# A new hand-kept order of 2,562 operations for an attention-then-mixture kernel on one Trainium2 core

## The chip, the core and the metric

One core of a Trainium2 chip runs the whole program. Its engines are TensorE (matrix products into PSUM, PE in the profile, with its weight loads apart as PEld), VectorE (DVE), ScalarE (ACT), GpSimd (POOL) and SyncE (SP), which here only issues transfers. The metric is the device time in microseconds, the median of several runs.

## What is computed

The reference has two parts, for a batch of 8, 8 heads of 64, and 576 positions:

```python
q_d, k_d, v_d = (mean over groups of 4 positions of q, k, v)
out_up = repeat(softmax(q_d k_d^T / 8) v_d, 4)                    # down-sampled attention
out_local = softmax(where(|i - j| < 4, q k^T / 8, -1e9)) v        # local attention
x = (out_up + out_local), heads side by side                      # [8, 576, 512]
logits = x @ w_gate; the two largest of 4 experts, softmax over them -> w
for e in range(4):
    q, k, v = x @ wq[e], x @ wk[e], x @ wv[e]                     # 512 -> 64
    ye = causal_softmax(q k^T / 8) @ v @ wo[e]                    # 64 -> 512
    out += w[e] * ye            # only where e is one of the two
```

## The kernel before

The work is cut into three stages for each batch element b. Stage 1 works on four pairs of heads c: `local` (the local scores, L515, 20 small products of 64x64 tiles), `down` (the down-sampled scores, L588), softmax work on VectorE, ScalarE and GpSimd (L518 to L536 and L591 to L609), transposes `tp` (L383), `o1` and `o1d` (products with v, L650 to L662) and `up` and `x` on VectorE (L667, L670). x is then split into a high and a low part, `xh` (L675) on ScalarE, and `xl` and `xt` (L676, L678) on VectorE or GpSimd. For b = 0 the down-sampled v is made on TensorE (`vd_mm`, L573), for the others on VectorE or GpSimd (`vd`, L567 and L568). Stage 2 projects x to q, k and v by dense 128-row products in three parts, high by high, high by low and low by high (L693, L739, L748; for q of b = 0 and its first pair of experts pair by pair at L708), and stage 3 does the causal attention and the output (L852 to L1011). Results leave PSUM by copies at L325 (ScalarE) and L327 (VectorE).

Each operation is written once as an entry of a plan, with the engines that may do it ("GV": GpSimd or VectorE; "AV": ScalarE or VectorE). A table of numbers, `SEQ`, decides everything else: the number divided by 4 says which operation comes next, the rest says which of its engines takes it, and -1 stands for a warm-up, a product of zeros (L472) that writes a PSUM buffer which nobody reads. Each engine gets its instructions in the order of the table and keeps it; it waits only for what an instruction needs. Seven more warm-ups (L360) stand ahead of the table.

```python
        for x in SEQ:
            o = self.ops[x // 4] if x >= 0 else self.filler()
            o.which = x % 4 if x >= 0 else 0
            o.who = o.eng[o.which]
            out.append(o)
```

TensorE products on plain float32 tiles of 64 rows (stage 1, scores, and the products with v) are issued as two passes each, so an operation of 20 such products is 40 matmuls and 40 weight loads in the trace; transposes and the dense products are issued once.

Of the kernel before, what the change touches and what calls it, by code (L numbers as in the profile page):

```python
# [17 lines left out]
    0, 173, 2112, 4, 177, 24, 136, 140, 189, -1, 192, 197, 120, 268, -1, 124, 232, -1, -1, -1, -1, -1, 200, 20,  # L18
    1148, 144, 64, 84, 92, 236, 149, 152, 240, -1, 204, 208, 244, 272, 88, 96, -1, -1, -1, 285, -1, -1, -1, -1, -1,
    -1, -1, -1, 288, 292, 156, 160, 164, 169, 220, 416, 8, 12, 68, 72, 296, 216, 413, 180, 185, 376, 380, 301, 304,  # L20
    76, 214, 312, 320, 429, 364, 16, 80, 572, 248, 316, 324, 384, 432, 437, 252, -1, -1, 128, 132, 360, 532, 536,
    440, 256, 328, 332, 336, 340, 260, 344, 308, 388, 540, -1, 568, 392, 464, 468, 348, 353, 264, 445, 28, 48, 52,
    356, 504, 544, 396, 400, 404, 773, 448, 408, -1, -1, 276, 280, 508, 776, 456, 460, 585, 588, 736, 740, 592, 744,
    720, 472, 476, 548, 40, 44, 480, 484, 552, 488, 556, 516, 224, 724, 228, 420, 32, 454, 620, 596, 424, 624, 708,
    897, 560, 748, 752, 492, 601, 604, 610, 36, 612, 617, 520, 712, 840, 844, 784, 788, 793, 796, 628, 632, 368,
    372, 576, 580, 56, 636, 564, 660, 664, 668, 672, 812, 756, 848, 760, 901, 909, 640, 496, 500, 801, 804, 852,
    764, 768, 644, 648, 656, 652, 810, 912, 1061, 512, 996, 676, 680, 60, 684, 688, 816, 1024, 1028, 1065, 917, 856,
    920, 925, 692, 696, 704, 781, 1032, 876, 880, 884, 936, 940, 944, 832, 524, 948, 1073, 1076, 1080, 1084, 528,
    952, 956, 960, 1000, 716, 1196, 1237, 700, 888, 1036, 964, 1200, 860, 1204, 904, 1208, 1088, 864, 868, 872, 928,
    968, 1092, 1040, 1044, 892, 1168, 100, 112, 104, 1332, 1336, 836, 1233, 1049, 972, 980, 1508, 828, 824, 820,  # L30
    1069, 1212, 1216, 1220, 1052, 1340, 1056, 1224, 1228, 976, 1152, 1156, 728, 732, 1172, 1008, 1012, 1513, 984,
    988, 1436, 934, 1098, 1160, 992, 1108, 1112, 1100, 1104, 1245, 1248, 1548, 1552, 1556, 1560, 1252, 1256, 1261,
    1432, 1753, 1564, 1004, 1460, 1464, 1568, 1572, 1468, 1756, 1576, 1264, 1268, 1580, 1164, 1272, 1277, 1292,
    1344, 1180, 1520, 1524, 1116, 1120, 1124, 1496, 1472, 1476, 1528, 1532, 1348, 1352, 1128, 1132, 1136, 1480,
    1537, 1540, 1356, 1544, 1484, 1488, 1384, 1284, 1500, 1296, 1288, 1300, 1176, 1184, 1360, 1364, 1368, 1592,
    1388, 1504, 1584, 1144, 1492, 1588, 1648, 1644, 2073, 1241, 1141, 1596, 1608, 1612, 1600, 1604, 1304, 1308,
    1312, 1316, 1616, 1392, 1396, 1765, 1768, 1320, 1716, 1328, 1324, 1620, 1624, 1720, 1728, 1016, 1020, 1400,
    1404, 1408, 2077, 1773, 1776, 1724, 1780, 1784, 1672, 1676, 1412, 1416, 1516, 1790, 1372, 1376, 1820, 2128,
    1680, 1732, 1736, 1740, 1744, 1420, 1424, 1280, 1429, 117, 1380, 1824, 2132, 1828, 1832, 2016, 1708, 1629, 1792,
# [1091 lines left out]
```

## Time and profile before

| | us |
|---|---|
| median of 3 runs (453.13 to 455.3) | 453.43 |
| span of the profiled execution | 451.9 |
| TensorE busy | 441.2 |
| VectorE busy | 362.5 |
| ScalarE busy | 346.1 |
| GpSimd busy | 301.2 |

The profiled execution is one more run; of its own time the profile gives the span, from the first to the last instruction, which lies 1.5 us under the median of the runs. The ends of matmuls are modelled, so that a TensorE that the profile calls busy can still be slower than at its best; idle time of an engine that others wait for is what costs.

### The profile page before, as it was taken

The page shows a single profiled execution, that of the slowest core. Times are in us where ns is not written, and L with a number is a line of the kernel's source. Part 1 is how long each engine was busy: PE and PEld are TensorE (multiplying, and loading weights), DVE is VectorE, ACT ScalarE, POOL GpSimd, SP SyncE. Part 2 cuts the span into 40 slices and gives each one's busy share as a digit, 9 for nine tenths or more (in the row PEclk, how much of TensorE's full clock was granted, in tenths as well). Part 3 has the DMA queues.
Part 4 walks back from the last instruction along what each step waited for, and adds up shares of the span by engine and source line. Part 5 has one row for each costly group of instructions (what it writes and reads, how often), then busy time and mean ns, then how long its engine had stood idle before and what let it go on. Part 6 is the DMA issues. An engine that isn't in the chain of part 4 may idle for free.

```text
span 451.9 us, 20317 instructions
## 1 busy us (share of the span) xinstructions
PE 441.2 (98%) x8374; PEld 401.8 (89%) x8375; DVE 362.5 (80%) x1020; ACT 346.1 (77%) x1099; POOL 301.2 (67%) x485
## 2 busy tenths in 40 slices
PE   8998999999999999999999999999999999999997
PEld 4787999989999889998899898999999999998876
DVE  8997989896859999777988999895897768445782
ACT  7985899687968898756867888775997687456783
POOL 6997878768867888665764776765984863304320
PEclk9998999999999999999999999999999999999999
DMA  8966537433344544543334432443272200200113
GB/s 251 281 191 188 169 99 212 123 112 83 89 141 137 155 126 136 158 141 89 113 108 160 118 99 65 133 140 92 62 220 63 70 1 4 80 28 14 52 57 106
DMA packets 44300, 52.70 MB, mean 117 GB/s; under 512 B 4144, under 2 KB 27184, under 8 KB 44208
## 3 DMA queue, kind: packets, MB, share of 16 engines
q1 hardware_dynamic: 44208, 51.40, 38.1%
q8 instruction: 66, 1.08, 1.0%
q14 instruction: 26, 0.21, 0.1%
HBM read 40.90 MB, written 9.44 MB: 111 GB/s over the span
## 4 chain that ended last, share of the span: by engine, by line
PE 87%; DVE 4%; DMA 4%; issue 2%; SPq 1%; ACT 1%; DVEq 0%; ACTq 0%
PE pj L693 20%; PE pv L739 10%; PE po L989 10%; PE sq L852 9%; PE o L966 8%; PE tq L383 6%; PE tp L383 5%; PE sc L515 4%; PE o L650 4%; PE scd L588 3%; DMA lv<-in_v_dram 3%; PE pv L748 2%; PE o L657 2%; PE po L1011 1%; PE o L970 1%
## 5 line engine op out<-in xcount | busy, mean ns | idle before, releaser
L875 ACT ACTIVATE pr<-pr,pst 128x384 f32<-128x384 f32 (+8 forms) x144 | 80.0, 558 | 13.3 <-DVE pst L872 12.6
L883 POOL TENSOR_SCALAR pr<-pr,pst,gt 128x64 f32<-128x64 f32 (+8 forms) x97 | 65.9, 687 | 16.2 <-DVE pst L880 12.0
L693 PE MATMUL pj<-xh,wqk_h 128*128 128x320 f32 (+1 forms) x248 | 74.8, 302 | 0.0
L693 PE MATMUL pj<-xh,wqk_l 128*128 128x320 f32 (+1 forms) x248 | 72.8, 293 | 0.0
L693 PE MATMUL pj<-xl,wqk_h 128*128 128x320 f32 (+1 forms) x248 | 72.7, 293 | 0.0
L872 DVE CUSTOM_DVE_ANT_0 pr<-sq,causal_t 128x384 f32<-128x384 f32 (+8 forms) x144 | 63.8, 484 | 5.2 <-PE sq L852 4.7
L852 PE MATMUL sq<-k,q 64*64 64x256 f32 (+6 forms) x768 | 52.2, 370 | 0.0
L693 PEld LDWEIGHTS pj<-xh,wqk_h 128*128 128x128 f32 x248 | 46.5, 188 | 2.5 <-issue 0.6
L693 PEld LDWEIGHTS pj<-xh,wqk_l 128*128 128x128 f32 x248 | 46.5, 188 | 0.0
L693 PEld LDWEIGHTS pj<-xl,wqk_h 128*128 128x128 f32 x248 | 46.5, 187 | 0.0
L978 POOL TENSOR_TENSOR ol<-oc,oh 128x256 fp32r<-128x256 f32 (+1 forms) x27 | 22.1, 822 | 32.4 <-ACT oh L977 22.6
L852 PEld LDWEIGHTS sq<-k,q 64*64 64x64 f32 x768 | 32.9, 133 | 7.0 <-issue 0.3
L598 ACT ACTIVATE dp<-scd,dst 128x144 f32<-128x144 f32 x96 | 35.2, 376 | 3.4 <-DVE dst L593 2.7
L739 PE MATMUL pv<-wvg_h,xh 128*128 128x260 f32 x128 | 37.0, 289 | 0.0
L739 PE MATMUL pv<-wvg_l,xh 128*128 128x260 f32 x128 | 36.1, 282 | 0.0
L739 PE MATMUL pv<-wvg_h,xl 128*128 128x260 f32 x128 | 36.1, 282 | 0.0
L676 POOL TENSOR_TENSOR xl<-x,xh 128x576 fp32r<-128x576 f32 x22 | 32.4, 1473 | 4.5 <-ACT xh L675 4.0
L536 POOL TENSOR_TENSOR lp<-lp,lst 128x640 f32<-128x640 f32 x24 | 31.9, 1336 | 4.4 <-DVE lst L535 3.7
L383 PE MATMUL tq<-ident,pr 64*128 64x64 f32 x736 | 33.2, 228 | 1.4 <-DVE pst L872 0.6
L989 PE MATMUL po<-oh,wo_h 128*128 128x256 f32 (+1 forms) x112 | 34.0, 304 | 0.0
L989 PE MATMUL po<-oh,wo_l 128*128 128x256 f32 (+1 forms) x112 | 33.0, 294 | 0.0
L383 PEld LDWEIGHTS tq<-ident,pr 64*128 64x128 f32 x736 | 27.1, 138 | 6.5 <-issue 2.6
(182 smaller groups left out, 1438.8 us busy)
## 6 DMA issues: line engine op xcount, KB each, us to landing
lv<-in_v_dram SPq DMA_DIRECT2D x64, 160.0 KB, 3.7
lq<-in_qT_dram SPq DMA_DIRECT2D x32, 292.0 KB, 3.5
lk<-in_kT_dram SPq DMA_DIRECT2D x32, 292.0 KB, 3.9
out_dram<-ot SPq DMA_DIRECT2D x28, 288.0 KB, 2.3
lr<-in_v_dram SPq DMA_DIRECT2D x28, 256.0 KB, 3.2
lr<-in_v_dram SPq DMA_DIRECT2D x56, 32.0 KB, 3.0
wst<-in_wqk_dram SPq DMA_DIRECT2D x1, 1024.0 KB, 9.1
vx<-vg SPq DMA_DIRECT2D x8, 128.0 KB, 2.6
```

Source lines behind the costliest of these rows:

```text
L383: T.transpose(ps()[:, 512 * x + z[x]:512 * x + z[x] + 64], data[r, 0:128], ident[r, r])
L536: op("l_nrm", "GV", (pool_tt(n), dve(n)), lambda e: eng[e].tensor_tensor(p(), p(), st[:, :, 2:3].to_broadcast([128, NT, W]), op=OP.mult), ...
L598: A.activation(p()[:, t, :], scs()[:, at * t:at * t + SD], AF.Exp, bias=st[:, t, 4:5], scale=1.0 / 128.0, accum_out=st[:, t, 0:1])
L676: op("xl", "GV", (1360, dve(576)), lambda e: eng[e].tensor_tensor(xl(), x(), xh()[:, 0:S].bitcast(F32), op=OP.subtract), r=[x, (xh, 0)], w ...
L693: T.matmul(ps()[:, H0 + n0:H0 + n1], ww[:, c, w0 + 128 * p:w0 + 128 * p + 128], xx[b, c]()[:, n0:n1], start=(i == 0), stop=(i == 3 * NP - 1))
L739: T.matmul(ps()[:, at:at + 260], xx[b, c]()[:, 128 * t:128 * t + 128], ww[:, c, :], start=(i == 0), stop=(i == 3 * NP - 1))
L852: T.matmul(pss[x][0]()[halves[e ^ turned(t)], at_of[x] + at + to:at_of[x] + at + to + n1 - n0], q()[r, 64 * t:64 * t + 64], k()[r, n0:n1], ...
L872: op("s_max", "V", dve(n) + 4, lambda x=x, t=t, n=n, src=src: V.tensor_tensor_reduce(rows_of[t], src(), causal_t[:, S - 64:S + 256] if t = ...
L875: op("s_exp", "A", 281 + n / 1.2, lambda x=x, t=t, n=n: A.activation(rows_of[t], rows_of[t], AF.Exp, bias=st[:, x, 4:5], scale=-1.0, accum ...
L883: op("s_nrm", "GV", (327 + n / 1.2 + max(0, n - 384) * 1.1, 189 + n / 1.92), lambda g, x=x, t=t, n=n: eng[g].tensor_scalar(rows_of[t], row ...
L966: T.matmul(obs[x]()[r, q0:q1], vg()[kr, j, 64 * (2 * p + e):64 * (2 * p + e) + 64], pt()[kr, e, j, q0:q1], start=j == 0, stop=j == len(job ...
L989: T.matmul(ps()[:, H1 + n0:H1 + n1], ww[:, p, 128 * c:128 * c + 128], xx[b, p]()[:, n0:n1], start=(i == 0), stop=(i == 5))
```

## The change

Only the table `SEQ` changes. It has 2,562 entries in place of 2,586: the same operations, in a new order, and none of the 24 entries of -1. Of the operations, 202 go from the first engine of their list to the second, 142 from the second to the first, and 14 otherwise to or from a third. With the table seven lines shorter, line numbers after it are seven lower in the changed kernel.

```diff
 SEQ = (
-    0, 173, 2112, 4, 177, 24, 136, 140, 189, -1, 192, 197, 120, 268, -1, 124, 232, -1, -1, -1, -1, -1, 200, 20,
+    4, 0, 136, 177, 124, 173, 120, 220, 8, 12, 140, 216, 188, 192, 197, 144, 272, 269, 232, 16, 236, 360, 284, 200,
...
```

The choices of engine that move most: s_nrm (L883) from 97 on GpSimd and 47 on VectorE to 84 and 60; q_ev (the copy of q out of PSUM) from 13 on ScalarE and 3 on VectorE to 6 and 10; wo_ev (the copy of the output) from 28 and 8 to 20 and 16; v_ev from 14 and 2 to 11 and 5; xl from 22 on GpSimd and 10 on VectorE to 19 and 13; xt from 29 and 3 to 21 and 11; o_lo (L978) from 27 and 5 to 21 and 11; kd (L551 on VectorE, with L553) from 18 on GpSimd and 14 on VectorE to 13 and 19; and the other way vd from 17 on GpSimd and 11 on VectorE to 21 and 7, and qd from 13 and 19 to 17 and 15.

The first place is TensorE's queue at the very start, from the first local scores (`sc`) on. Before, warm-ups (`wu`) stand between them:

```order
L515 MATMUL sc<-lk,lq 64x64 x20
L588 MATMUL scd<-kd,qd 64x144 x6
L472 LDWEIGHTS zero
L472 MATMUL wu<-zero 128x512
L472 LDWEIGHTS zero
L472 MATMUL wu<-zero 128x512
L515 MATMUL sc<-lk,lq 64x64 x20
```

And now:

```order
L508 MATMUL sc<-lk,lq 64x64 x20
L581 MATMUL scd<-kd,qd 64x144 x6
L508 MATMUL sc<-lk,lq 64x64 x20
L581 MATMUL scd<-kd,qd 64x144 x6
L566 MATMUL pv<-lv,pool 128x128 x7
L508 MATMUL sc<-lk,lq 64x64 x20
L376 MATMUL tp<-ident,dp 128x64 x10
```

The warm-ups are gone, so that the real work follows directly, and the first `vd_mm` (`pv`) stands ahead of the third local scores; before, it stood behind 19 warm-ups.

The second place is TensorE's queue some 110 instruction rows later, where the last head pair of b = 0 is done (`o_870`, in the new table `o_804`) and the first projection (`pj`) begins. Before:

```order
L650 MATMUL o_870<-pt,lv 64x58 x16
L650 MATMUL o_870<-pt,lv 64x56 x4
L657 MATMUL o_870<-pd,vd 64x144 x4
L660 MATMUL o_870<-pd,vd 64x2x48
L662 MATMUL o_870<-pd,vd 64x48
L660 MATMUL o_870<-pd,vd 64x2x48
L662 MATMUL o_870<-pd,vd 64x48
L515 MATMUL sc<-lk,lq 64x64 x20
L708 MATMUL pj<-xh,wqk_h 128x320
L708 MATMUL pj<-xh,wqk_l 128x320
```

And now:

```order
L566 MATMUL pv<-lv,pool 128x128 x7
L581 MATMUL scd<-kd,qd 64x144 x6
L643 MATMUL o_804<-pt,lv 64x58 x16
L643 MATMUL o_804<-pt,lv 64x56 x4
L508 MATMUL sc<-lk,lq 64x64 x20
L650 MATMUL o_804<-pd,vd 64x144 x4
L653 MATMUL o_804<-pd,vd 64x2x48
L655 MATMUL o_804<-pd,vd 64x48
L653 MATMUL o_804<-pd,vd 64x2x48
L655 MATMUL o_804<-pd,vd 64x48
L701 MATMUL pj<-xh,wqk_h 128x320
L701 MATMUL pj<-xh,wqk_l 128x320
```

The last local scores ahead of the projection have moved in front of the `o1d` products (L657 to L662), and the last `vd_mm` now stands shortly ahead of them.

The third place is SP's queue of loads at the start. Before:

```order
L489 DMA lk<-in_kT_dram 128x584
L488 DMA lq<-in_qT_dram 128x584
L489 DMA lk<-in_kT_dram 128x584
L455 DMA wst<-in_wvg_dram 128x4x260
L489 DMA lk<-in_kT_dram 128x584
L499 DMA lv<-in_v_dram 64x5x128 x2
```

And now:

```order
L482 DMA lk<-in_kT_dram 128x584
L481 DMA lq<-in_qT_dram 128x584
L482 DMA lk<-in_kT_dram 128x584
L481 DMA lq<-in_qT_dram 128x584
L482 DMA lk<-in_kT_dram 128x584
L492 DMA lv<-in_v_dram 64x5x128 x2
```

The load of the weights for v and the gate (`in_wvg`) has left the first six loads; it now stands 13 rows further down, behind the weights for q and k.

## Rows read from the trace of the kernel before

**Rows 1.** The page: span, busy time of each engine, and the instruction queue's transfers.

```profile
span 451.9 us, 20317 instructions
PE 441.2 (98%) x8374; PEld 401.8 (89%) x8375; DVE 362.5 (80%) x1020; ACT 346.1 (77%) x1099; POOL 301.2 (67%) x485
...
q8 instruction: 66, 1.08, 1.0%
```

**Rows 2.** Busy time by stretch: bounds: length, busy (instructions) by engine, clock, DMA share, GB/s.

```profile
0.00:4.50 4.50, 3.20 (x11) 0.95 (x11) 2.94 (x14) 3.71 (x9) 2.95 (x24) 1.00 0.58 182
4.50:22.00 17.50, 16.68 (x338) 11.94 (x339) 16.92 (x36) 14.84 (x53) 15.25 (x25) 1.00 1.06 295
22.00:37.50 15.50, 12.40 (x381) 11.19 (x378) 13.27 (x31) 14.20 (x47) 14.98 (x19) 1.00 0.69 190
37.50:45.00 7.50, 7.50 (x165) 7.08 (x165) 5.40 (x11) 2.80 (x10) 4.88 (x6) 0.77 0.64 182
45.00:100.00 55.00, 55.00 (x1092) 51.09 (x1090) 51.45 (x141) 46.88 (x147) 43.02 (x60) 1.00 0.48 140
100.00:200.00 100.00, 99.94 (x1990) 93.40 (x1989) 82.09 (x233) 81.77 (x267) 77.13 (x125) 1.00 0.43 126
200.00:300.00 100.00, 98.58 (x1917) 91.44 (x1917) 88.06 (x250) 77.18 (x244) 66.17 (x103) 1.00 0.40 121
300.00:400.00 100.00, 99.97 (x1773) 93.48 (x1773) 71.00 (x206) 70.06 (x226) 61.87 (x100) 1.00 0.23 71
400.00:448.60 48.60, 47.80 (x732) 41.20 (x726) 31.39 (x106) 34.26 (x105) 14.94 (x29) 1.00 0.14 50
```

**Rows 3.** TensorE's waits: us in total, times, longest.

```profile
PE sc L515 <- issue: 1.7, 1, 1.7
...
PE tp L383 <- issue: 1.1, 1, 1.1
```

**Rows 4.** TensorE's timeline: start, length, instructions, [idle before <-releaser].

```profile
23.17 0.40 PE L383 MATMUL tp<-ident,lp 64*128 64x64 f32 x5 [1.07 <-issue]
...
37.50 0.56 PE L515 MATMUL sc<-lk,lq 64*64 64x64 f32 x19 [1.68 <-issue]
...
38.55 0.28 PE L708 MATMUL pj<-xh,wqk_h 128*128 128x256 f32 x1
...
39.65 0.42 PE L708 MATMUL pj<-xh,wqk_l 128*128 128x256 f32 x1
```

**Rows 5.** VectorE's timeline at the same two places, and the last `x` of b = 0.

```profile
24.28 0.62 DVE L591 TENSOR_REDUCE scd<-scd 128x3 f32<-128x432 f32 x1 [0.92 <-PE scd L588]
...
38.10 0.82 DVE L518 SCALAR_TENSOR_TENSOR lp<-sc,lmask 128x640 f32<-128x640 f32 x1 [1.83 <-PE sc L515]
...
39.63 0.74 DVE L670 SCALAR_TENSOR_TENSOR x<-up,o 128x576 f32<-128x576 f32 x1
```

**Rows 6.** The page's group of the warm-ups, as TensorE's lines show them.

```profile
L472 PE MATMUL wu<-zero 128*128 128x512 bf16 x23 | 6.2, 381 | 0.4 <-DMA lv<-in_v_dram 0.3 <-PE scd L588 0.2
```

**Rows 7.** VectorE's and GpSimd's groups by shape: busy us, mean ns | idle before.

```profile
L327 DVE COPY q<-pj 128x576 f32<-128x576 f32 x3 | 2.3, 754 | 1.0 <-PE pj L693 1.0
L883 DVE TENSOR_SCALAR pr<-pr,pst,gt 128x256 f32<-128x256 f32 x7 | 3.4, 483 | 0.0
L567 DVE TENSOR_TENSOR lr<-lr 128x512 f32<-128x512 f32 x11 | 8.4, 762 | 0.7 <-DMA lr<-in_v_dram 0.7
L568 DVE TENSOR_TENSOR vd<-lr 128x256 f32<-128x256 f32 x11 | 7.3, 666 | 0.4
```

**Rows 8.** Waits of TensorE's weight loads between 45 and 448 us, the longest two.

```profile
PEld tq L383 <- issue: 2.6, 12, 0.5
PEld sc L515 <- DVE oc L975: 0.9, 1, 0.9
```

**Rows 9.** The chain that ended last, its pieces of load time at the start.

```profile
6.57 8.25 DMA lv<-in_v_dram
14.83 5.00 DMA lv<-in_v_dram
```

273 rows, old and new, of the table SEQ are left out of this document.

## The prediction

> **What bounds the kernel now.** I read the page first: TensorE is busy 441.2 of 451.9 us, 98%, VectorE 80%, ScalarE 77%, GpSimd 67% [rows 1]. A new order cannot take products away, so the gain can only lie where TensorE stands idle, or where it is busy with something that is no work. Next I read the busy time by stretch, to see where that is [rows 2]. Between 45 and 448.6 us TensorE is idle 0.06, 1.42, 0.03 and 0.80 us, together 2.3 us of 403.6. In the first 45 us it is another picture: 16.68 of 17.5 us busy, but with 23 of the 24 warm-ups, worth 6.2 us [rows 6], in it; then 12.40 of 15.5; then 7.5 of 7.5, but at a mean granted clock of 0.77. So the start holds nearly all that is to be had, and it is VectorE's there: 16.92 of 17.5 us busy, then 13.27 of 15.5.
>
> The list of TensorE's waits gives the largest two holes a name: 1.7 and 1.1 us, both with the releaser "issue", which is no other engine [rows 3]. The timeline puts them at 22.1 to 23.17 and 35.82 to 37.50 us, in the middle of one operation each (5 of 10 transposes, 19 of 40 matmuls were still to come) [rows 4], so that no input can be what was missing. 22 + 677 = 699 instructions of TensorE stand before 22.0 us and 1458 before 37.5 us [rows 2]: 759 apart, close to three times 256. The instruction queue made 66 transfers of 1.08 MB together, 16.4 KB each, for 16,749 instructions of TensorE, 254 each [rows 1]. I read both holes as TensorE at the end of a block of instructions whose successor had not come. VectorE feels them at once: it is idle 0.92 us before L591 and 1.83 us before L518 [rows 5].
>
> After the second hole the granted clock falls: in 37.5 to 45 us it is 0.77 in the mean [rows 2], and the same 128x256 product takes 0.28 us at 38.55 and 0.42 us at 39.65 [rows 4]. This is a piece of about 3.4 us at the lower of two levels (1.2 in place of 2.4 GHz), right after 1.68 us of idleness.
>
> **The change, part by part.**
>
> *Holes at block ends in the start.* I counted the new queue, with two passes where the trace has two: the end near instruction 705 falls between transposes and the local scores of b = 1 (small products again), the one near 1473 into the first dense projection, which before came just after it. In the new queue a `vd_mm` of 28 instructions, 128 columns wide, also stands at the start of the block ahead. So I take the second hole as gone, 1.68 us of TensorE that VectorE, with 1.83 us, pays in full, and of the first a third: 2.0 us gained in all. The bounds are 2.75 us gained (both gone, 1.07 + 1.68) and none (two others come).
>
> The Trainium skill, in "Runtime: NRT & Kernel Launch", section "Instruction fetch mechanics", says that crossing into the next block of 256 instructions costs one queue update that is mostly hidden. By that this part would be worth nothing and the sum would end 2.0 us higher. The trace disagrees at two of 65 ends, with 1.07 and 1.68 us, and agrees at most others.
>
> *The lower clock after the second hole.* (1 - 0.77) x 7.5 = 1.7 us of full clock were lost in 37.5 to 45 us, where TensorE is busy throughout [rows 2]. With the hole goes what came before the fall. Gain 1.7 us, bounds 0 and 1.7.
>
> *The 24 warm-ups.* They lie in the stretch where VectorE is busy 16.92 of 17.5 us [rows 2], so their own 6.2 us are hidden behind VectorE, and taking them out gains nothing directly (bounds 0 and the 0.6 us that VectorE is idle there). But without them TensorE is idle more: in 4.5 to 22 us it is busy 16.68 - 6.2 = 10.5 of 17.5 us [rows 2, 6], and the only fall in the trace follows idleness. What this costs is not in the trace of before. From below it is nothing, as VectorE sets the pace; from above all of the work from 4.5 to 37.5 us, 10.5 + 12.4 = 22.9 us, runs at half the clock and takes 45.8 us in place of 33.0, 12.8 us more. Nearest is the one fall seen, 1.7 us; I take two such falls, half of each hidden behind VectorE: 1.7 us lost.
>
> *VectorE's work in the start.* Up to the last `x` of b = 0, which ends at 40.37 us [rows 5], VectorE has 67 operations in place of 64. Out go one xl, one l_nrm, one l_sub, one qd, one vd_ev and some small ones, in come one kd, one qd, one l_max, one vd_ev, two xt and four small ones; by the means of their kinds some 4.7 us go and 4.1 us come. Gain 0.6 us, bounds 0 and 1.2.
>
> *The loads in the start.* The chain of waits runs through the loads of v for 8.25 and 5.00 us [rows 9]. With the 520 KB of `in_wvg` out of the way of the first of them, at 295 GB/s [rows 2] it lands up to 1.8 us sooner; the second has some 230 KB less ahead, 0.8 us. VectorE's queue stands beside it with 16.92 of 17.5 us [rows 2], so I take 0, bounds 0 and 0.8 gained. The weights for v are needed only after the first q and k, and have more than ten microseconds.
>
> *The rest, 45 to 448.6 us.* Gain at most the 2.3 us that TensorE is idle, and something of the waits of its weight loads, the longest group of which is 2.6 us in 12 [rows 8]. Against that stands what VectorE takes over: 7 copies of q and 8 of the output at 0.754 us, 11.3 us; 13 s_nrm at about 0.49 us, 6.4 us; o_lo, xl, xt, kd and v_ev some 14 us; less 4 vd at 0.762 + 0.666 = 1.43 us, 5.7 us, and qd and the sums with eps, some 4 us [rows 7]. That is about 22 us more, 385 of 451.9 us or 85%. It has the room: 355 - 292.6 = 62.4 us idle in 45 to 400 us [rows 2]. The tightest stretch is 45 to 100 us, with 3.55 us free; its share of the 22 us, by its share of VectorE's time (51.45 of 362.5), is 3.1 us. So it stays just under its limit, and I take 1.0 us gained, less than half of the 2.3; bounds 2.3 + 2.6 = 4.9 gained and 3.1 lost, if that stretch has twice its share.
>
> *Sum.* 451.9 - 2.0 - 1.7 + 1.7 - 0.6 - 1.0 = 448.3 us of span; with the 1.5 us by which the median of the runs lies over the profile, 449.8 us.
>
> **The rivals.** *The plan's waits shrink too*: the stretch after 45 us gives its bound, 4.9 us in place of 1.0, and the time is 445.9 us. For it speaks that one wait of 0.9 us there hangs on VectorE behind a long instruction [rows 8]; against it, that VectorE gets more to do, not less.
>
> *No change*: two other block ends fall into small products, the holes and the fall of the clock come again elsewhere (2.0 + 1.7 us back), and the time is 453.5 us. For it speaks that the end near 705 still lies between small products; against it the dense projection at 1473.
>
> *Slower: the clock falls in the start.* With no warm-ups TensorE goes to the lower level again and again until the projections begin. If half of the 22.9 us of work runs there and all of it shows, 11.4 us are lost in place of 1.7, and the time is 459.5 us; from 7.6 us lost on it is slower than before by over 0.5%, and I price this case in the middle, at 457.5 us. For it speaks that idleness of 1.68 us came before the only fall, and that idleness of this size will be common; against it, that TensorE's share of work in 22 to 37.5 us, with hardly a warm-up in it, was 12.40 of 15.5 us at a clock of 1.00 up to its end [rows 2], and that VectorE's queue hides what TensorE loses. The Trainium skill, in "TensorE: Matmul & The Clock Gate", section "What's actually happening", says that the throttled state is the default and that activity releases it; by that this rival is what the missing warm-ups bring, and the fall at 39 us agrees.
>
> **How the numbers follow.** The forecast, about 447.5 to 451.1 us, has 0.40; the shorter waits, 444 to 447.5, 0.16; no change, 451.2 to 455.7, 0.25; the slower start 0.19. 0.5% of 453.43 is 2.3 us, about what a measurement of this kernel can tell from no change, so faster is 0.40 + 0.16 = 0.56, same 0.25, slower 0.19. The range from 444.5 to 456.0 us leaves out the far ends of the second and the fourth case, some 0.05 and 0.13. The forecast by itself is 449.8 us.
>
> **What would show it.** In the profile after: no wait of TensorE on "issue" over 1 us at the start beside at most one; VectorE's wait on the local scores near 38 us gone; the last `x` of b = 0 ending at 36 to 39 us in place of 40.37; the dense projections beginning that much sooner; the granted clock below 1.00 in one or two stretches before 37 us; VectorE near 385 us busy; the rest, from the first projection to the end, as long as before within 2 us. The prediction is wrong if the granted clock stays at half for ten microseconds or more of the start, if new holes on "issue" stand in the stretch after 45 us, or if TensorE there waits for VectorE by several microseconds.

## The result, and the profile after

The changed kernel takes 458.21 us in the median of 12 runs (455.02 to 462.29), the kernel before, beside it on the same chip, 454.32 us. The ratio is 1.0068, interval [1.0042, 1.0095]; in another set of runs (after_2, below) it is 1.0092 [1.0067, 1.0117]. A ratio is worked out from the single runs and leaves out those in a slower state of the chip (here the one of 462.29 us), so that it is not quite the quotient of the two medians. So the change makes the kernel about 0.8% or 3.6 us slower, and the prediction was wrong.

The profiled execution is a long one of the changed kernel's, with a span of 460.0 us; the middle span of the runs is 456.5. The page, by engine, for [rows 1]:

```profile
span 460.0 us, 20255 instructions
...
PE 441.0 (96%) x8351; PEld 401.5 (87%) x8351; DVE 375.8 (82%) x1062; ACT 333.3 (72%) x1075; POOL 288.5 (63%) x466
...
q8 instruction: 66, 1.08, 0.9%
```

VectorE has gained 13.3 us of work, ScalarE and GpSimd have lost about as much each. TensorE is as busy as before, though 24 warm-ups are gone. The same stretches as in [rows 2]:

```profile
4.50:22.00 17.50, 11.24 (x291) 9.77 (x292) 11.97 (x27) 10.94 (x42) 11.56 (x18) 0.92 1.08 274
22.00:37.50 15.50, 14.01 (x377) 12.38 (x379) 14.48 (x36) 13.23 (x41) 12.76 (x14) 0.98 0.80 224
37.50:45.00 7.50, 6.34 (x182) 5.68 (x174) 7.10 (x15) 5.88 (x18) 6.78 (x9) 1.00 0.22 58
45.00:100.00 55.00, 54.18 (x1095) 49.76 (x1090) 53.34 (x137) 43.20 (x142) 42.15 (x58) 1.00 0.44 126
100.00:200.00 100.00, 96.98 (x1827) 89.58 (x1820) 83.57 (x234) 74.30 (x247) 66.03 (x104) 0.98 0.46 129
200.00:300.00 100.00, 99.80 (x1941) 91.65 (x1944) 86.28 (x250) 74.75 (x239) 68.01 (x107) 1.00 0.38 111
300.00:400.00 100.00, 99.41 (x1873) 92.22 (x1866) 80.64 (x232) 72.90 (x241) 61.76 (x104) 1.00 0.29 91
```

Two stretches stand out. In 4.5 to 22 us VectorE does 11.97 us in place of 16.92, though it set the pace there. And between 100 and 200 us TensorE is idle for 3.0 us, where it was idle for 0.06. TensorE's waits, for [rows 3], tell why:

```profile
PE sc L508 <- issue: 3.6, 2, 3.4
PE o L959 <- issue: 1.8, 1, 1.8
PE sc L508 <- DMA lq<-in_qT_dram: 1.4, 1, 1.4
PE pv L566 <- DMA lv<-in_v_dram: 1.2, 1, 1.2
...
PE pj L701 <- issue: 1.0, 1, 1.0
```

The waits on "issue" sum to 6.8 us, with a small one of 0.4; before it was 2.8. TensorE's timeline, for [rows 4], shows the three large ones, each in the middle of an operation (the number in brackets is the idle time before the row, with what ended it):

```profile
14.72 0.57 PE L508 MATMUL sc<-lk,lq 64*64 64x64 f32 x22
18.68 0.50 PE L508 MATMUL sc<-lk,lq 64*64 64x64 f32 x17 [3.39 <-issue]
...
40.45 0.39 PE L701 MATMUL pj<-xl,wqk_h 128*128 128x256 f32 x1 [1.01 <-issue]
...
172.74 0.70 PE L959 MATMUL o<-ptb,vg 64*64 64x320 f32 x3
175.26 2.43 PE L959 MATMUL o<-ptb,vg 64*64 64x320 f32 x27 [1.82 <-issue]
```

The first one is felt on VectorE at once, as in [rows 5]; it has nothing to do for 3.95 us:

```profile
21.03 0.46 DVE L660 TENSOR_REDUCE up<-o 128x144 f32<-128x288 f32 x1 [3.95 <-PE o L655]
```

What was late is seen in the transfers by queue, in 12 to 14 us, first before, then after, and in 16 to 18 us after (packets, MB, share of the 16 engines):

```profile
q1 hardware_dynamic: 566, 0.46, 109.9%
q8 instruction: 1, 0.02, 4.3%
```

```profile
q1 hardware_dynamic: 678, 0.42, 116.4%
```

```profile
q1 hardware_dynamic: 384, 0.75, 102.9%
q8 instruction: 1, 0.02, 3.5%
```

The first block of TensorE's instructions that is fetched during the run (q8) starts at 12.11 us before, at 16.13 us after; TensorE passes the block end after which this fetch comes at about the same time, 7.6 and 8.2 us. All 16 engines are then full of loads, in both. TensorE uses up what it has at 15.0 us and stands until 18.68, that is 2.55 us after the fetch began. Lower clock follows both long waits: 0.92 in 4.5 to 22 us, and 0.83 in 170 to 180 us.

A second profiled execution of the same kernel, after_2 (span 456.2 us, near the middle), has the first fetch at 12.01 us and no wait near 15 us; at 172 us the wait is 0.69 us (a pause of 1.4 us between two weight loads), at 22 to 24 us there is one of 1.1. So the ends of the blocks stay, and what is waited at them changes from one execution to the next. The clock falls here too, in 4.5 to 22 us, with no wait on issue in that stretch:

```profile
4.50:22.00 17.50, 14.41 (x320) 12.57 (x322) 13.41 (x31) 11.36 (x43) 12.37 (x19) 0.80 1.08 267
```

All its waits on issue together are 2.9 us, about the 2.8 of before, and yet its span is 4.3 us longer. The sum of these waits alone therefore doesn't give the loss; where in the run they stand matters too, as the table below shows.

### The profile page after: what moved, and what is told of

Same layout as the page of the kernel before. It is cut to its first block, busy times and chain, and to the rows that moved or that the text cites. A ratio compares the mean times of both kernels' runs of the same rounds, so it can differ in the third digit from the quotient of the medians.

```text
span 460.0 us, 20255 instructions
## 1 busy us (share of the span) xinstructions
PE 441.0 (96%) x8351; PEld 401.5 (87%) x8351; DVE 375.8 (82%) x1062; ACT 333.3 (72%) x1075; POOL 288.5 (63%) x466
## 3 DMA queue, kind: packets, MB, share of 16 engines
q8 instruction: 66, 1.08, 0.9%
## 4 chain that ended last, share of the span: by engine, by line
PE 83%; DVE 7%; issue 3%; POOL 3%; DMA 3%; ACT 1%; SPq 1%; POOLq 0%
PE pj L686 21%; PE po L982 9%; PE pv L732 9%; PE sq L845 8%; PE o L959 7%; PE tq L376 5%; PE tp L376 5%; PE o L643 4%; PE sc L508 4%; PE scd L581 3%; PE pv L741 2%; PE o L650 2%; PE po L1004 1%; DMA lv<-in_v_dram 1%; PE pv L566 1%
## 5 line engine op out<-in xcount | busy, mean ns | idle before, releaser
L868 ACT ACTIVATE pr<-pr,pst 128x192 f32<-128x192 f32 (+8 forms) x144 | 80.1, 560 | 13.2 <-DVE pst L865 12.6
L865 DVE CUSTOM_DVE_ANT_0 pr<-sq,causal_t 128x320 f32<-128x320 f32 (+8 forms) x144 | 64.4, 482 | 9.7 <-PE sq L845 9.3
L876 POOL TENSOR_SCALAR pr<-pr,pst,gt 128x192 f32<-128x192 f32 (+8 forms) x84 | 59.7, 718 | 14.4 <-DVE pst L873 10.9
L529 POOL TENSOR_TENSOR lp<-lp,lst 128x640 f32<-128x640 f32 x23 | 29.5, 1281 | 15.3 <-DVE lst L528 12.7
L845 PEld LDWEIGHTS sq<-k,q 64*64 64x64 f32 x768 | 31.9, 134 | 7.1 <-issue 0.2
L971 POOL TENSOR_TENSOR ol<-oc,oh 128x320 fp32r<-128x320 f32 (+1 forms) x21 | 17.9, 854 | 31.4 <-ACT oh L970 31.4
L959 PE MATMUL o<-ptb,vg 64*64 64x320 f32 (+2 forms) x512 | 32.9, 383 | 1.8 <-issue 1.8
L982 PE MATMUL po<-ol,wo_h 128*128 128x256 f32 (+1 forms) x112 | 32.9, 294 | 0.0
L508 PE MATMUL sc<-lk,lq 64*64 64x64 f32 x1280 | 27.7, 224 | 5.1 <-issue 3.6
```

The costliest lines, as they stand in the source:

```text
L508: T.matmul(sc()[halves[h ^ (t // 5)], 512 * (t // 5) + W * i:512 * (t // 5) + W * i + W], q()[r, z:z + 64], k()[r, z:z + W], start=True, s ...
L529: op("l_nrm", "GV", (pool_tt(n), dve(n)), lambda e: eng[e].tensor_tensor(p(), p(), st[:, :, 2:3].to_broadcast([128, NT, W]), op=OP.mult), ...
L845: T.matmul(pss[x][0]()[halves[e ^ turned(t)], at_of[x] + at + to:at_of[x] + at + to + n1 - n0], q()[r, 64 * t:64 * t + 64], k()[r, n0:n1], ...
L865: op("s_max", "V", dve(n) + 4, lambda x=x, t=t, n=n, src=src: V.tensor_tensor_reduce(rows_of[t], src(), causal_t[:, S - 64:S + 256] if t = ...
L868: op("s_exp", "A", 281 + n / 1.2, lambda x=x, t=t, n=n: A.activation(rows_of[t], rows_of[t], AF.Exp, bias=st[:, x, 4:5], scale=-1.0, accum ...
L876: op("s_nrm", "GV", (327 + n / 1.2 + max(0, n - 384) * 1.1, 189 + n / 1.92), lambda g, x=x, t=t, n=n: eng[g].tensor_scalar(rows_of[t], row ...
```

## The experiments

Four theories. **A**: the loss is waits of TensorE at block ends, and the falls of the clock behind them. **B**: the missing warm-ups cost it. **C**: the engine choices, with VectorE's load. **D**: the new order as such. Each kernel ran in rounds with the kernel before. The profiles are of one execution each. Medians and ratios:

| label | median us | before us | ratio, 95% interval |
|---|---|---|---|
| b_nofill | 453.97 | 454.44 | 0.9993 [0.9965, 1.0021] |
| a_fill | 457.56 | 454.44 | 1.0061 [1.0036, 1.0086] |
| a_tiny | 456.71 | 454.44 | 1.0054 [1.0029, 1.0080] |
| a_choice_b | 516.66 | 454.44 | 1.1391 [1.1337, 1.1444] |
| ba_start | 455.52 | 453.83 | 1.0041 [1.0020, 1.0062] |
| ab_start | 459.04 | 453.83 | 1.0120 [1.0097, 1.0143] |
| a_wless | 456.74 | 453.83 | 1.0063 [1.0037, 1.0090] |
| after_2 | 458.17 | 453.83 | 1.0092 [1.0067, 1.0117] |
| b_split | 457.57 | 455.00 | 1.0049 [1.0020, 1.0077] |
| ba_nofill | 456.39 | 455.00 | 1.0034 [1.0006, 1.0062] |
| ab_fill | 460.36 | 455.00 | 1.0118 [1.0073, 1.0163] |
| a_act | 465.37 | 455.00 | 1.0213 [1.0166, 1.0259] |
| b_split5 | 457.62 | 454.93 | 1.0063 [1.0038, 1.0088] |
| a_split3 | 463.49 | 454.93 | 1.0188 [1.0161, 1.0216] |
| a_split5 | 465.45 | 454.93 | 1.0237 [1.0211, 1.0263] |
| a_best | 466.30 | 454.93 | 1.0262 [1.0231, 1.0292] |
| a_ld | 456.93 | 452.92 | 1.0101 [1.0073, 1.0128] |
| a_mend | 456.52 | 452.92 | 1.0063 [1.0040, 1.0087] |

### The warm-ups

```diff
 SEQ = (
-    0, 173, 2112, 4, 177, 24, 136, 140, 189, -1, 192, 197, 120, 268, -1, 124, 232, -1, -1, ...
+    0, 173, 2112, 4, 177, 24, 136, 140, 189, 192, 197, 120, 268, 124, 232, ...
```

*b_nofill.* 

> The kernel before with its 24 warm-ups taken out and nothing else changed. Theory A (the loss of the change is waits of TensorE for its next block of instructions, and the falls of the granted clock that follow such waits): each block end moves to 48 instructions later in the program's work, so the two waits of before (1.07 and 1.68 us) come elsewhere, and the time goes with the new sum of waits on issue: with 5 us of them in place of 2.8 about 457 us, with 2.8 about 454; the granted clock stays 1.00 wherever no such wait stands ahead. Theory B (the missing warm-ups cost it, by TensorE's idleness): 4 us slower than before, about 458, with a granted clock below 1.00 in the first 37 us without a wait on issue ahead of it. Theory C (the engine choices, VectorE's load): the time of before, 454.3 within 1.

*a_fill* (24 entries of -1 put into the new table). 

> The changed kernel with 24 full warm-ups put back at the places of the work where the kernel before has them. Theory A: the block ends move by 48 instructions, so the waits on issue of 3.39, 1.0 and 1.8 us stand at other work and change size; the time goes with them: 453 to 458 us, and where a wait over 1.5 us is gone, so is the fall of the clock behind it. Theory B: 4 us back, about 454, by a granted clock of 1.00 through the first 37 us, whatever the waits on issue do. Theory C: no change, about 458 within 1.

*a_tiny* changes the warm-up itself as well:

```diff
-        o.fn = lambda: T.matmul(ps()[:, :512], zero[:, :128], zero, start=True, stop=True)
+        o.fn = lambda: T.matmul(ps()[:, :2], zero[:, :128], zero[:, :2], start=True, stop=True)
```

> The changed kernel with 24 products of 2 columns in place of 512 at the places of the warm-ups, so that the block ends lie where they lie with full warm-ups, and TensorE has hardly any more to do. Theory A: the same time and the same waits on issue as with full warm-ups, within 1.5 us. Theory B: as the changed kernel without warm-ups, about 458 us, and 4 us longer than with full ones, with a granted clock below 1.00 in the start. Theory C: no change, about 458 within 1.

Without warm-ups the kernel before takes the same time, 0.9993, and with them the changed one is hardly faster. The clock did fall without them, in b_nofill to 0.80 and 0.89 (columns as in [rows 2]); the second fall stands behind a wait on issue of 2.1 us at 25.4 us, the first behind none:

```profile
4.50:22.00 17.50, 13.64 (x310) 12.03 (x310) 14.89 (x34) 13.32 (x48) 14.30 (x23) 0.80 1.08 282
22.00:37.50 15.50, 13.26 (x356) 12.22 (x360) 13.71 (x32) 13.42 (x43) 13.58 (x18) 0.89 0.62 158
```

But that time was hidden. B falls. That a_fill and a_tiny, with the same block ends, agree within their intervals speaks for no more than that: their waits on issue in one execution each are 2.3 and 4.2 us.

The falls of the clock, the second half of A, don't explain the loss by themselves either. The granted clock is 0.997 in the mean of 102 runs of the kernel before and 0.993 in 18 runs of the changed one; but it is 0.990 in the 12 runs of b_nofill, which is as fast as before.

### The engine choices

The diffs of this section and the next are in short form; the tables themselves are numbers. *a_choice_b* (the new order, each number with the last digit of the old choice) and *a_act* (20 numbers changed by one):

```diff
-    x = 4 * op + new_choice          # of every operation
+    x = 4 * op + old_choice          # a_choice_b: all but the flips of `down`; a_act: q_ev and wo_ev that went to VectorE
```

> The changed kernel's order with the engine choices of the kernel before (VectorE, ScalarE or GpSimd for each elementwise operation). Theory A: the instructions of TensorE are the same in the same order, so the block ends stay and with them the waits on issue of about 3.4, 1.0 and 1.8 us: within 1.5 us of the changed kernel, 456.5 to 459.5. Theory C: the loss goes away, about 454, with VectorE near 362 us busy in place of 376. Theory B: no change.

> The changed kernel with 20 of VectorE's new copies (8 of q, 12 of the output) given back to ScalarE, which had them before; the order is the changed one. Theory A: nothing of the waits on issue changes: 458 within 1, with VectorE near 361 us busy. Theory C (VectorE's load): 2 to 4 us faster, 454 to 456.

a_choice_b takes 516.66 us: an order made for one set of choices is of no use with the other, and so this kernel told nothing of C. a_act is the clean one. VectorE falls from 375.8 to 364.3 us, as meant, and the time rises by 1.3% over the changed kernel's 1.0080 (the mean of its two ratios). So giving VectorE's load back doesn't help. This tells against C only in the form in which ScalarE gets what VectorE loses.

### Start or rest

Here the table is one order up to the first `scores` over the whole sequence, at 54 to 56 us, and the other behind it (ba: start of before; ab: changed start):

```diff
-SEQ = before
+SEQ = before[:first scores] + [x for x in after if x not in before[:first scores]]     # ba_start
+SEQ = the same without the -1                                                        # ba_nofill
+SEQ = after[:first scores] + [x for x in before if x not in after[:first scores]]      # ab_start
+SEQ = a_fill[:first scores] + the same rest as ab_start                              # ab_fill
```

> The order and engine choices of the kernel before, warm-ups included, up to the first scores over the whole sequence (54 us), then the rest in the order and with the choices of the changed kernel. Theory A (block ends and the clock falls behind waits on them): the start is that of before with its waits of about 1.1 and 1.7 us; the block ends of the rest lie at other work than in the changed kernel, so that the 1.8 us wait and the fall near 172 us should be gone: 454 to 455.5 us. Theory D (the new order or choices are slower in the steady part, whatever the blocks): as slow as the changed kernel, 457 to 459. Theory B (the start's idleness): as before, 454.

> The kernel with the start of before and the rest of the changed one, now without the 24 warm-ups: the block ends of the rest fall where they do in the changed kernel. Theory A: the wait at the block end near 170 us is back, with 1.4 to 2.5 us, and a fall of the clock behind it where it is over 1.5: 456.5 to 458 us, 1 to 2.5 more than with the warm-ups (455.5). Theories B and D: as with the warm-ups, 455.5 within 0.7, since taking them out of the kernel before changed nothing.

> The reverse: the changed kernel's order and choices, without warm-ups, up to the first scores over the whole sequence (56 us), then the rest in the order and with the choices of the kernel before. Theory A: the start with its waits on issue of 3 to 5 us in all, and a rest without large ones: 456 to 457.5 us. Theory B: as the changed kernel, about 458. Theory D: as before, 454 within 1.

> The kernel with the changed start and the rest of before, now with 24 warm-ups in the start: the block ends of the rest fall where they do in the kernel before. Theory A: the waits on issue of 0.95 us near 73 us and 1.25 us near 351 us go, and the time falls by 1.5 to 3 us from 459, to 456 to 457.5. Theories B and D: 459 within 0.7 (or, by B, back to 454.5 with the warm-ups).

The new rest behind the old start costs 0.41% and, without warm-ups, 0.34%: 1.5 to 1.9 us, about half of the loss. That the other half belongs to the start doesn't follow from this, since the changed rest needn't cost the same behind another start; the traces under *after_2* put most of it into the rest. The ab kernels can't be read as the start's price: both have a seam that costs time, in ab_start (then ab_fill, much the same)

```profile
62.41 0.41 PE L686 MATMUL pj<-xh,wqk_h 128*128 128x320 f32 x1 [2.39 <-DVE vg L320]
```

```profile
65.38 0.63 PE L687 MATMUL pj<-xh,wqk_h 128*128 128x320 f32 x1 [2.42 <-DVE vg L321]
```

In ba_nofill the waits come back at the very ends of the changed kernel's rest, as A has it (pauses of 0.67, 0.83 and 0.93 us near 164, 170 and 349 us, and none of these in ba_start), but small, and the time didn't move. In ab_fill the two near 73 and 351 us went, as expected, and the time didn't follow there either.

What the new rest costs without large waits at block ends is, as far as I found it, small things. Half a microsecond is the very end. Before, the last two copies stand on ScalarE; after, the last piece is made straight behind the one before it in the same tile, and ScalarE's copy waits for VectorE's (before; then after_2):

```profile
448.73 0.37 ACT L325 COPY ot<-po 128x256 f32<-128x256 f32 x1 [0.33 <-PE po L1011]
```

```profile
453.03 0.37 ACT L318 COPY ot<-po 128x256 f32<-128x256 f32 x1 [1.73 <-DVE ot L320]
```

From TensorE's last start to the end of the span it is 4.0 us in after_2 and 3.5 before.

### Fewer bytes in the start

```diff
-                st(), src.rearrange("(c p) j -> p c j", p=128)), w=[st], alloc=[st])
+                st()[:, :1] if less else st(), (src[:128] if less else src).rearrange("(c p) j -> p c j", p=128)), w=[st], alloc=[st])
```

*a_wless.* 

> The changed kernel, loading only a quarter of the weights for q and k and of those for v (some 390 KB in place of 1544 KB), each chunk of the sum then using that quarter; so the projections are not the reference's, the amount of computing is unchanged. At about 295 GB/s some 3.9 us of transfers are out of the first 20 us. Theory A (the fetch of the next block stands behind the loads): the first fetches of instruction blocks start up to 3.9 us sooner, the wait on issue of 3.39 us near 15 us shrinks under 1.5 us, and the time falls by 2 to 4 us to 454 to 456. Rivals B and D: the clock and the steady part are as they were, and the time stays at 457 to 458 but for what VectorE's waits for data give, at most 1 us.

The first fetch began at 15.21 us, hardly sooner than 16.13, and 2.9 us of wait stood near 15 us again: other loads filled the room, and the engines were nearly as full (0.98 in 4.5 to 22 us, where it was 1.08). This run says nothing for A, and against the simple form of it, in which the bytes of the weights are the delay.

*after_2* is the changed kernel once more. 

> The changed kernel once more, to see which of its waits come back. Theory A: waits on issue at the same block ends (the second, near 15 us; the sixth, near 39 us; the one near 172 us) but of other lengths, since what they stand behind is when a fetch gets through; where one is 1.5 us or longer, the granted clock falls behind it; over the runs a lower mean clock goes with a longer span, at about 1.8 us for 0.004. Theory D: the time after 55 us is the same within 1 us with and without such waits, and 4 us longer than before.

The waits at the ends near 39, 172 and 351 us came back, and one near 23 us came in place of that near 15. Over the 18 runs of the changed kernel a granted clock lower by 0.004 goes with a span longer by 1.1 us, not 1.8, and loosely (correlation -0.42). D expected the time after the start to be the same with and without large waits; it isn't. The first row of this table is the time from the start of the matmul that has 6,900 behind it to that of the last one, worked out from the records of each trace, for the order of the changed kernel. The second row adds up TensorE's pauses in that time which stand at a block end and end within 4 us of the start of the fetch that they wait for (pauses over 0.35 us between two weight loads). The split kernels, a_ld, a_mend and a_best (a_split5 with another end) come below.

| us | a_fill | a_tiny | a_ld | a_mend | a_wless | after_2 | a_split3 | after | a_split5 | a_best |
|---|---|---|---|---|---|---|---|---|---|---|
| rest | 373.7 | 373.9 | 374.4 | 375.6 | 376.1 | 377.0 | 377.3 | 379.1 | 379.5 | 380.1 |
| pauses | 0 | 0.4 | 0.7 | 1.6 | 2.4 | 2.6 | 1.7 | 4.1 | 6.5 | 7.3 |

The order of before takes 373.3 (before, with 0.5 of pauses), 373.6 (b_nofill, 0.8), 374.1 (b_split5, 1.8) and 376.8 (b_split, 4.4). With ends that lie well the new rest is nearly as short as the old one, and what it takes more goes with the pauses, but for a_split3. The matmul from which this counts starts at 75.2 us in before and in after_2, at 76.8 in after, and at 75.4 to 76.3 in a_ld, a_mend and a_wless. So in after_2, whose span is near the median, the start costs nothing; of its 4.3 us, 3.8 lie in this rest and 0.5 behind the last matmul. a_fill and a_tiny lost in the start what they won here: the count starts at 78.3 and 77.1 us in them.

### The same work, other block ends

A warm-up of 512 columns is cut into 3 products of 170 or 5 of 102:

```diff
-        o.fn = lambda: T.matmul(ps()[:, :512], zero[:, :128], zero, start=True, stop=True)
+        nth[0] += 1
+        o.fn = lambda n=nth[0]: [T.matmul(ps()[:, :170], zero[:, :128], zero[:, :170], start=True, stop=True) for _ in range(3)] \
+            if n <= 22 else T.matmul(ps()[:, :512], zero[:, :128], zero, start=True, stop=True)
```

*b_split* (the kernel before). 

> The kernel before, with 22 of its 24 warm-ups each split from one product of 512 columns into three of 170: the same columns on TensorE, the same order, choices and work, but 88 instructions more before the last product of the first 20 us, so that every block end behind them falls on other work. Theory A (the place of the block ends sets the time): I went through the trace of before with the ends set 88 instructions back, and a fetch that takes 4.6 us to start in the first 45 us and 1.3 to 2.6 behind, and 2.45 us from its start to TensorE: waits of about 3 us near 18 us, 0.9 near 25, and some 2.3 us in the rest (0.8 near 244, 1.3 near 348), in place of the 1.8 that the same reckoning gives for before: 4 us longer, with falls of the clock behind the longest, about 457 to 459 us. Theory D (the new order or its choices, not the blocks): 454 within 1. Theory B: 454.

*b_split5.* 

> As b_split, but 22 warm-ups split into five products of 102 columns: 176 instructions more than before, at the same columns. Theory A (the place of the block ends): the same reckoning from the trace of before gives waits of 1.5 us in all (0.9 near 24 us, 0.6 near 347) against 1.8 for before and 6.4 for b_split: as before, 454 within 1, and 2 to 4 us faster than b_split. Rival E (every added instruction costs): b_split lost 2.4 us by the median with 44 more products, so twice as much here, 459.

*a_split3* and *a_split5* (a_fill). 

> The changed kernel with the 24 warm-ups put back (a_fill), 22 of them split into three products of 170 columns: 88 instructions more than a_fill. Theory A: by the reckoning from the traces of a_fill and a_tiny the waits grow by about 3 us (one of 2.4 to 2.9 near 17 us): 459 to 461, against 457.6 for a_fill. Rival E: 460. Theory D (the order as such): as a_fill, 457.6 within 0.7.

> The changed kernel with warm-ups, 22 of them split into five products of 102 columns: 176 instructions more than a_fill. Theory A: waits of 0.2 to 0.6 us in all by the reckoning, against 0.7 to 2.3 for a_fill and a_tiny: 455 to 456.5, faster than a_fill (457.6) and 3 to 5 us faster than a_split3. Rival E: 462. Theory D: 457.6 within 0.7.

In b_split the largest wait came where the reckoning put it, near 18 us. In the rest there were pauses of 0.5 and 0.9 us near 250 and 353, as reckoned but smaller, and of 1.9 and 1.0 near 152 and 179, where it had next to nothing:

```profile
22.28 0.39 PE L661 MATMUL o<-pd,vd 64*64 64x144 f32 x1 [3.31 <-issue]
...
154.22 0.45 PE L519 MATMUL sc<-lk,lq 64*64 64x64 f32 x12 [1.66 <-issue]
```

The old order lost 0.49%, 2.2 us, by nothing but 44 more products that add no columns. The whole change lost 3.6. a_split3 has its large wait, of 3.02 us, in front of a warm-up at 22.09 us, where 2.4 to 2.9 us near 17 were expected. But it takes 463.49 us, more than this wait explains, and b_split5 and a_split5, which by the reckoning should have been fast, were not: b_split5 had a wait of 3.7 us near 20 (and one of 2.4 near 48 that the profile puts down to GpSimd's `vd`, at a block end too), a_split5 waits of 7.1 us in all.

```profile
PE o L648 <- issue: 3.5, 2, 2.6
PE sc L513 <- issue: 2.4, 3, 1.0
PE o L658 <- issue: 1.2, 1, 1.2
```

So two things are shown. The number of instructions ahead of a block end moves time, at equal work and order: in b_split the last 6,900 matmuls are the same as before, in the same order, and no instruction is added among them, yet they take 3.5 us more, with 3.9 us more of pauses at block ends. And I can't reckon from the trace of one kernel at which ends another will wait. Twice as many instructions cost the old order no more (0.49 and 0.63%, intervals that overlap); in the new one they did (1.88 and 2.37%), so that rival E, a price for each instruction in the start, isn't excluded there. The products themselves are hardly more work: 20 of the 102-column ones take 1.23 us by their starts in a_split5, 0.31 for five, against 6.2 / 23 = 0.27 for a whole one [rows 6], by which estimate all 22 would cost 0.9 us.

### Three transfers moved

```diff
-    ..., 3920, 2688, 3924, ..., 3980, 5428, 4176, ..., 4296, 2704, 3644, ..., 3992, 4496, ...
+    ..., 3920, 3924, ..., 3980, 4176, ..., 4296, 3644, ..., 3992, 2688, 5428, 2704, 4496, ...
```

*a_ld.* 

> The changed kernel with three transfers of 868 KB together (two output stores of 288 KB, one load of k) moved in SyncE's queue from 166 to 171 us to behind the load that is issued at 175.8; nobody needs them before 190 us. Theory A (a fetch that stands behind transfers comes late, and the wait is what is left of it): at the block end near 172 us the fetch, which began 5.7 to 6.9 us after TensorE came near the end before, begins 2 to 4 us after it, the wait of 1.4 to 2.5 us shrinks under 0.6, no fall of the clock follows there, and the time falls by 1 to 3 us from 458.2, to 455.5 to 457. If the short block alone makes it: the wait stays at 1.4 us or more, and the time at 458 within 1.

*a_mend* (a_ld, and the last ten entries in another order):

```diff
-    10192, 10196, 10176, 10236, 10232, 10181, 10200, 10184, 10240, 10244
+    10232, 10176, 10181, 10184, 10192, 10196, 10200, 10236, 10240, 10244
```

> As a_ld, and the last ten operations in the other order (the last piece is copied by ScalarE beside VectorE's copy of the piece before). Theory A: 0.5 us less than a_ld, 455 to 456.5: what is left against before, up to 2 us, are the larger waits on issue in the start and some 1 us of small waits in the rest. Theory D (the order as such): 457.7 within 1.

*a_best* was a_split5 with that end. 

> As a_split5, and the last ten operations in another order, so that the last piece that TensorE makes is copied by ScalarE while VectorE copies the piece before the last. In the changed kernel 1.1 us pass from TensorE's last product to the end of the last copy, in the kernel before 0.6. Theory A: 0.5 us faster than a_split5, 454.5 to 456, which is as fast as before or up to 0.4% slower. Theory D: as a_split5 less 0.5.

The fetch before the end near 172 us did what A says. In 172 to 174 us of the changed kernel, the fetch starts only there, in the middle of the burst; in a_ld, it has started in 168 to 170:

```profile
q1 hardware_dynamic: 253, 0.47, 88.2%
q8 instruction: 1, 0.02, 3.1%
```

```profile
q1 hardware_dynamic: 321, 0.55, 92.5%
q8 instruction: 1, 0.02, 3.0%
```

I count a fetch as due where TensorE is 64 instructions ahead of the end of the block before; this is a counting point of mine, and the shortest time from it to a fetch is 0.7 us in all these traces. From there the fetch begins 6.85 and 5.68 us later in the two executions of the changed kernel, 4.39 and 4.88 in a_ld and a_mend. TensorE stood there 2.5 and 1.4 us (between two weight loads), and now not at all and 0.62. The stretch of 170 to 180 us in after, after_2 and a_ld, each with TensorE's busy time first:

```profile
170.00:180.00 10.00, 8.18 (x184) 6.59 (x186) 6.21 (x16) 5.83 (x17) 2.48 (x2) 0.83 0.61 191
```

```profile
170.00:180.00 10.00, 9.28 (x240) 7.34 (x233) 8.15 (x22) 7.36 (x27) 4.56 (x6) 1.00 0.47 149
```

```profile
170.00:180.00 10.00, 10.00 (x261) 8.79 (x254) 9.55 (x25) 7.78 (x28) 5.75 (x7) 1.00 0.46 135
```

But the medians hardly follow: a_ld is 1.2 us under after_2 and at 1.0101 of its own before, a_mend at 1.0063; neither lies clearly under the changed kernel's 1.0068 and 1.0092. The profiled execution of a_ld, 455.60 us, is the shortest of its six. In these executions the fetch comes sooner with the transfers moved; that the wait is worth 2 us in the middle run is not shown. The end is mended too: in a_best the span ends 3.4 us after TensorE's last start, in a_split5 4.0; the median of a_best doesn't show it. None of these kernels beats the one before; b_nofill is equal to it.

## Why the prediction was wrong

**Holes at block ends in the start**: this step failed. It counted where two known ends would fall, 705 and 1473, and took 2.0 us gained. It left out the end before them, at instruction 449, which waits for the first fetch of the run (the waits of TensorE's queue counted in, these ends stand 256 instructions apart). In seven profiled executions of the changed start without warm-ups (after, after_2, a_wless, a_act, a_ld, a_mend, ab_start), this fetch begins at 14.1 to 16.3 us in five, and TensorE waits 1.6 to 3.4 us for it; in the two others it begins at 12.0 and 12.5, with no wait. In the start of before (before, b_nofill, ba_start, ba_nofill: 11.1 to 13.0 us) and in the changed one with 24 products put back (a_fill, a_tiny, ab_fill: 11.6 to 12.4) it was never that late. Why it is late in the changed start isn't settled; a_wless excludes the bytes of the weights alone. The end at 1473 did fall into the dense projection, and still cost 1.01 us in the profile after and 0.6 in after_2 (before: 1.68): so a wait there was shorter and not hidden, as I had taken for granted. Up to the matmul that has 6,900 behind it, after_2 takes as long as before (75.2 us), and after 1.7 us longer.

The step also set the bounds too near: "none (two others come)" as the worst. Waits on issue over the whole run were 6.8 us in one execution and 2.9 in the other, against 2.8.

**The rest, 45 to 448.6 us**: this step failed most. It forecast 1.0 us gained (4.9 gained to 3.1 lost), and of block ends it said nothing, since there were hardly any waits there before. The rest takes more: with its own block ends 377.0 and 379.1 us for the last 6,900 matmuls, against 373.3 before, that is 3.8 and 5.8 us lost, with 2.6 and 4.1 us of pauses at block ends where there were 0.5; with other ends (a_fill) it takes 373.7. Behind the start of before it costs less in the median, 1.5 to 1.9 us by ba_start and ba_nofill. One of the prediction's own signs of being wrong, new holes on "issue" behind 45 us, is what came. The price of VectorE's load was seen rightly to be small: it rose by 13.3 us, not 22, and giving back 11.5 us of it made the kernel slower.

**The lower clock after the second hole**: wrong. The fall went from 37.5 to 45 us (now 1.00) and came back elsewhere: in after where the new waits stand, 0.92 in 4.5 to 22 us and 0.83 in 170 to 180 us; in after_2 in 4.5 to 22 us, 0.80, with no wait on issue there. So the gain of 1.7 us didn't come.

**The 24 warm-ups**: the sign of the mechanism was right, the clock does fall without them (0.80 in b_nofill), but the term is mis-sized: 1.7 us predicted, nothing measured (0.9993), since all of it lies beside other waits. **VectorE's work in the start** and **the loads** were taken as 0.6 and 0 gained. VectorE was busy 30.2 us between 4.5 and 37.5 us before [rows 2] and 26.5 after: it did less in that time because it waited. Its last `x` of b = 0 starts at 41.86 us in the long run profiled, at 40.37 in after_2, against 39.63 [rows 5]: later, where an end at 36 to 39 us was forecast. TensorE's waits for data, 1.4 us for a q and 1.2 for a v, are new.

**The rivals**: "slower start by falls of the clock" has nearly the right time (457.5), by luck: its reason, the missing warm-ups, cost nothing in b_nofill. "No change" named the cause, other ends that fall into small products, and stopped at equal. The rival that was missing is that one with its real sizes: a first fetch that comes later than before, and an end in the steady part that meets a burst of transfers.

The prediction weighed the Trainium skill, "Runtime: NRT & Kernel Launch", section "Instruction fetch mechanics", by which crossing into the next block is mostly hidden. By that the sum would have been 2.0 us higher. This case's traces agree at most ends and disagree at two to seven of some 65 in each kernel, with waits on issue of 0.2 to 3.7 us each.

**What stays open**: by ba_start and ba_nofill the new rest carries about half of the loss, by the two traces of the changed kernel itself most or all of it; some 0.5 us of this is the very end, and the waits at block ends vary from run to run. How much of the median each wait carries I couldn't isolate: the two kernels that mended the one at 172 us weren't measurably faster. a_split3 and a_split5 lost 6 to 8 us against a_fill, 2.6 to 2.7 of it in the start; in the rest of a_split5 the pauses cover the loss, in that of a_split3 they don't (1.7 of 3.6 us).

## What to carry to other kernels

When a reorder moves instructions on an engine that runs thousands of them, go through all block ends and not only those where the trace shows a wait: at each, compare the time that the last block lasts with how late the next fetch may come while transfers are thick. And an order and its engine choices belong together: going back to the old choices in the new order cost 1.3% for 20 of them and 13% for all.

## What the runs showed of the hardware

- A block of instructions (16.4 KB) is fetched among the data's transfers: the profile counts both on the same 16 DMA engines, and with three transfers moved away the fetch before the end near 172 us came 0.8 to 2.5 us sooner. Counted as for a_ld, a fetch began 1.1 to 1.5 us after it was due at several ends where the engines were nearly idle (1.14 near 182 us after), and mostly 4 to 6 us late in the first 38 us, where they were full (8.8 for the first fetch of a_ld, which began at 16.30).
- TensorE went on 2.2 to 3.0 us after the start of the fetch it waited for, in nearly every such wait (2.55 us at 18.68 us in the changed kernel); longer, 3.4 to 4.0, mostly where the fetch itself took 1.6 us and more.
- Such waits stand at the same instructions in each execution of an order, with other lengths. In after, after_2 and a_ld the pause between two weight loads is 3.66, none and 2.03 us at instruction 449, and 2.5, 1.4 and none at 6849 (in a_ld with transfers moved).
